# Order of work at both ends of a fused retention and MLP kernel

## The chip, the cores and the metric

The kernel runs on one core of a Trainium2 chip. The metric is the device time of one execution in microseconds (us), the median of several runs. A core has five engines that run side by side, each working through its own instructions in order: TensorE (PE, matrix products, with PEld for its weight loads), VectorE (DVE), ScalarE (ACT), GpSimd (POOL) and SyncE (SP, which here issues nearly all transfers). Transfers can also be issued from ACT; they then stand among ACT's own instructions.

## The reference

```python
# q, k, v: (8, 8, 576, 64) float32; w_in: (512, 2048); w_out: (2048, 512)
scores = (q @ k.T) / sqrt(64)                  # per batch and head
gamma = 1 - 2 ** (-5 - head)                   # decay of a head
ret = scores * where(i >= j, gamma ** (i - j), 0)
x = (ret @ v), heads side by side              # 4608 tokens x 512
h = x @ w_in
g = h * erf(softplus(h))
out = g @ w_out                                # 4608 x 512
```

The weights arrive as 64-bit floats; the kernel rounds them to float32 itself.

## The kernel before, in words

**Attention in pieces.** The 4608 tokens are cut into 36 pieces of 128 tokens. Of each batch's 576 tokens four pieces are whole, and the last 64 of two batches share a ninth piece. A piece i goes through three functions, called stages. `transposes(i)` brings q and k to the layout with the head dimension on the partitions: for pieces 0 to 7 by PE (L314) and an ACT copy (L315), from piece 8 on by DVE (L308). It also issues the q (or q and k) load of piece i + 2. `scores(i)` makes the 16 small products of q and k (L324) and masks them on DVE into the tile sT. `outputs(i)` multiplies sT with the values (L338), adds the carried state of the batch (L349), and makes this piece's contribution kv to the state (L362). DVE adds kv to the old state (`sums`), and POOL multiplies the sum with the decay (L379, the new state; for a batch's first piece DVE does it). DVE scales the output into the tile x. It also issues the k and v loads of piece i + 3. The decay that belongs to a key's position is put into the values ahead of time: `weigh_values(i)` is one multiplication on POOL (L296), which must be done before L338 and L362 of that piece. Each function is called when its turn comes, and its instructions join their engines' queues in that order.

The list `stages` holds the order of these calls. In the loop over i it appends transposes(i + 1), outputs(i), scores(i + 1), and swaps neighbours for a few i. PC is 4, so four pieces make one chunk of 512 tokens; there are nine chunks.

**Weights.** `round_weights(n)` emits n steps of the rounding of one weight part: two ACT passes, four DVE passes (L242, L246, L250, L255), two POOL passes (L256, L257), after which the next part's load is issued. The first group's eight parts (four of w_in, four of w_out) are rounded while attention starts; the last step of a w_in or w_out set makes four sums on DVE.

**The MLP.** Both matrix products use seven half-size products in place of eight, with sums of operands (named A11, S1 to S4, ... and B11, T1 to T4, ...). The hidden dimension is cut into 4 groups; for each group all nine chunks pass. `First(g, c)` makes the hidden tile of one group and chunk, `Second` multiplies it with w_out and accumulates onto an output tile o that is kept in DRAM between groups. In a `Second` the products B11, T2, T1, B22 go into one PSUM accumulator, each on top of the last, and DVE or ACT reads it out between them (`take`); B21 has an accumulator of its own, T3 and T4 share a third (`add`). Each such product is eight matmuls (L551; L445 in `First`). The very first one is done plainly with eight products (`plain`, L499), mixed among attention's stages.

**The order at the start** is written out by hand in one string: a calls the next stage, p the next plain product, w loads two weight parts, s stores chunk 0 of x, a digit emits that many rounding steps. `keep_busy(2)`, after six of the first stages, multiplies the identity with itself to keep PE at work (L631). The string's end is followed by the rest of chunk 1 and the first products of chunk 1.

**The order at the end.** In the last two blocks there is no next `First` to put between the products. The second last block runs T2, T3, T1 (`middle`), then B22, T4 (`last`); the sums of the next block are made; then B11, B21 (`first`), and the last block runs `middle` and `last`. The results of the last group go straight to the output by `store`, one transfer per piece segment, all issued by SP. Every wait here comes from data: an accumulator that must be read before PE adds to it, a buffer that must be free, a transfer that must land.

Of the kernel before, what the change touches and what calls it, by code (L numbers as in the profile page):

```python
# [15 lines left out]
ALU = mybir.AluOpType  # L16
# [31 lines left out]
def kernel(  # L48
# [42 lines left out]
    def tt(out, in0, in1, op):  # L91
        nc.vector.tensor_tensor(out=out, in0=in0, in1=in1, op=op)  # L92
# [56 lines left out]

    load(0)  # L150
    cst = cpool.tile([P, CONST_COLS], FP32, name="cst")
    nc.scalar.dma_start(out=cst, in_=consts)
    ends = [0]
    for m in (H, NP * P, NP, P, H):
        ends.append(ends[-1] + m)
# [127 lines left out]
    def x_tile():  # L283
        return xpool.tile([P, n_dc + 3, TCH], FP32, tag="x", name="x")
# [12 lines left out]

    def transposes(i):
        t = live[i] = loaded.pop(i)
        if i < SQUARES:  # L300
            weigh_values(i + 1)
        for name in "qk":
            tT = t[name + "T"] = att.tile([P, NP, P], FP32, tag=name + "T", name=name + "T")
            if i >= SQUARES:
                for _, _, n, r0 in pieces[i]:
                    a = r0 // SQ * D
                    squares = t[name + "s"][:, :, a : a + n // SQ * D].rearrange("p h (a d) -> p h a d", d=D)
                    nc.vector.transpose(  # L308
                        out=tT[:, :, r0 : r0 + n].rearrange("p h (r a) -> p h a r", r=SQ), in_=squares[:, :, :, :SQ]
                    )  # L310
            else:
                pt = ps_at.tile([P, NP, P], FP32, tag="at", name=f"pt_{name}")
                for p in range(NP):
                    nc.tensor.transpose(pt[:, p, :], flat(t[name][:, 2 * p : 2 * p + 2, :]), ident)  # L314
                nc.scalar.copy(out=tT, in_=pt)  # L315
        load(i + 2, "q")
# [14 lines left out]
    def outputs(i):  # L331
        segments = pieces[i]
        t = live.pop(i)
        seen = [(kept[b], r0, n) for b, s0, n, r0 in segments if s0 > 0]
        o = ps_at.tile([P, NP, P], FP32, tag="at", name="o")
        for p in range(NP):
            for e in range(2):
                nc.tensor.matmul(  # L338
                    o[heads[e], p, :],
                    lhsT=t["v"][:, 2 * p + e, :],  # L340
                    rhs=t["sT"][:, e, p, :],
                    start=(p == 0),
                    stop=(not seen and p == NP - 1),
                    skip_group_check=True,
                )
        for state, r0, n in seen:
            for p in range(NP):
                for r in heads:
                    nc.tensor.matmul(  # L349
                        o[r, p, r0 : r0 + n],  # L350
                        lhsT=state[r, p, :],
                        rhs=t["qT"][r, p, r0 : r0 + n],
                        start=False,
                        stop=(p == NP - 1),
                        skip_group_check=True,
                    )
        b, s0, n, _ = segments[0]
        if n == P:
            kv = ps_at.tile([P, NP, D], FP32, tag="at", name="kv")
            for p in range(NP):  # L360
                for e in range(2):
                    nc.tensor.matmul(  # L362
                        kv[heads[e], p, :],
                        lhsT=t["k"][:, 2 * p + e, :],
                        rhs=t["v"][:, 2 * p + e, :],
                        start=(p == 0),
                        stop=(p == NP - 1),
                        skip_group_check=True,
                    )
            sums = kv  # L370
            if s0 > 0:
                sums = att.tile([P, NP, D], FP32, tag="sums", name="sums")
                tt(sums, kv, kept[b], ALU.add)

            if b % 2 == 0 and s0 + P + D == S:
                new = att.tile([P, NP, D], FP32, tag="last", name="last", bufs=1)
            else:
                new = att.tile([P, NP, D], FP32, tag="state", name="state")
            (nc.gpsimd if s0 > 0 else nc.vector).tensor_tensor(out=new, in0=sums, in1=gp, op=ALU.mult)  # L379
            kept[b] = new  # L380
        load(i + 3, "kv")
        weigh_values(i + 1)
        c, at = i // PC, i % PC * P
        if (0, c) not in x:
            x[0, c] = x_tile()
        by = gq[:, :, :n].unsqueeze(2).to_broadcast([P, NP, P // n, n])
        parts = [y.rearrange("p a (m i) -> p a m i", i=n) for y in (x[0, c][:, :NP, at : at + P], o)]
        tt(parts[0], parts[1], by, ALU.mult)

    stages = [(transposes, 0), (scores, 0)]  # L390
    for i in range(len(pieces)):
        stages += [(transposes, i + 1), (outputs, i), (scores, i + 1)]
        if i in (PC - 1, PC):
            stages[-3:-1] = stages[-2], stages[-3]
    stages = [(of, i) for of, i in stages if i < len(pieces)]
    done = [0]

# [4 lines left out]
    def after_chunk(c):  # L402

        return stages.index((outputs, (c + 1) * PC - 1)) + 1
# [31 lines left out]
    class First:  # L436
# [84 lines left out]
            for j, t in enumerate((self.t1, self.t2)):  # L521
                tt(t, t, self.s[:, j], ALU.mult)

        def sums(self):
            g11, g21, g12, g22 = (t[:, j] for t in (self.t1, self.t2) for j in range(2))
            s1, s2, s3, s4 = (self.s[:, i, j] for i in range(2) for j in range(2))
            tt(s1, g12, g22, ALU.add)
            tt(s2, s1, g11, ALU.subtract)
            tt(s3, g11, g12, ALU.subtract)
            tt(s4, g21, s2, ALU.subtract)  # L530

            self.left = {B11: g11, B21: g21, T2: s2, T3: s3, T1: s1, B22: s4, T4: g22}

    class Second:


        def __init__(self, first):
            self.of = first
            self.g, self.c = first.g, first.c
            self.end = (self.g, self.c) == (n_g - 1, n_ch - 1)  # L540

        def begin(self):
            self.o = opool.tile([P, 2, 2, D_MODEL], FP32, tag="o", name="o")
            if self.g > 0:
                nc.sync.dma_start(out=self.o, in_=od[self.c])

        def product(self, b, acc, start):
            left = self.of.left[b]
            for j in range(GP):
                for tp in range(2):  # L550
                    nc.tensor.matmul(  # L551
                        acc[:, tp, :],
                        lhsT=left[:, j * TH + tp * P : j * TH + (tp + 1) * P],
                        rhs=weights["wb", self.g][:, b, j, :],
                        start=(start and j == 0 and tp == 0),
                        stop=(j == GP - 1),
                        skip_group_check=True,
                    )
# [36 lines left out]
        def last(self):  # L595
            self.product(B22, self.a, False)
            self.take(0, 1, self.a, "scalar")
            self.store(0)
            if self.end:
                self.store(1, slice(OH, D_MODEL))  # L600
            yield
            self.product(T4, self.e, False)
            self.add(1, 0, self.e)
            self.store(1, slice(0, OH if self.end else D_MODEL))
            yield

        def store(self, half, os=slice(0, D_MODEL)):
            if self.g < n_g - 1:
                nc.sync.dma_start(out=od[self.c][:, half, :, os], in_=self.o[:, half, :, os])
            else:  # L610
                for tp in range(2):
                    for b, s0, n, r0 in pieces[self.c * PC + 2 * half + tp]:
                        nc.sync.dma_start(
                            out=out[b * S + s0 : b * S + s0 + n, os], in_=self.o[r0 : r0 + n, half, tp, os]
                        )

# [27 lines left out]
    products = firsts[0].plain()  # L644


    for j, what in enumerate("aaaawaaawaa4a1a5asa1a4pa5papapa5p4apa1p4apa5a5a"):
        if what == "a":
            attend(done[0] + 1)
        elif what == "p":  # L650
            next(products)
        elif what == "s":
            store_x(0)
        elif what == "w":
            load_weights()
            load_weights()
        else:
            round_weights(int(what))
        if j < 7 and what == "a":
            keep_busy(2)  # L660
    firsts[0].softplus()
    most[0] = before_chunk(3)
    attend(after_chunk(1))
    operands_x(0, 1)
    attend(done[0] + 1)
    for _ in firsts[1].first():
        attend(done[0] + 1)
        round_weights(2)
# [2 lines left out]
    for b, nxt in zip(blocks[1:], blocks[2:] + [None]):  # L671
# [23 lines left out]
        elif n + 1 < n_s:  # L695
            firsts[n + 1].erf()
            seconds[n + 1].begin()
            run(b.middle())
            firsts[n + 1].multiply()
            run(b.last())  # L700
            firsts[n + 1].sums()
            run(nxt.first())
        else:
            run(b.middle())
            run(b.last())


# [28 lines left out]
```

## Time and profile before

| | us |
|---|---|
| median of 5 runs | 1053.4 (1052.75 to 1054.94) |
| profiled execution | 1052.97 |
| its span in the trace | 1051.2 |
| PE busy | 1030.8 (98%) |
| DVE busy | 639.6 (61%) |
| ACT busy | 378.1 (36%) |
| POOL busy | 134.6 (13%) |
| mean granted clock of PE | 0.995 |
| share of PE in the chain that ended last | 93% |

The span runs from the first instruction to the last event; the 1.8 us around it belong to the execution but not to the trace. Busy times of an engine are sums over its instructions. Idle time of an engine that is not the bound costs nothing by itself.

### The profile page before, as it was taken

How to read it: one execution, taken by the hardware profiler on the slowest of the kernel's cores; microseconds unless marked ns; L12 is line 12 of the kernel's file. 1: busy time of each engine (PE TensorE's matmuls, PEld its weight loads, DVE VectorE, ACT ScalarE, POOL GpSimd, SP SyncE). 2: the span in 40 equal slices, each digit the busy share in tenths (PEclk: the TensorE clock that was granted, in tenths of full speed). 3: DMA queues.
4: the chain of work that ended last, by engine and by line, in shares of the span. 5: the costliest groups of instructions: out<-in, count | busy, mean ns of one | idle time of the engine just before them, and what ended most of it. 6: DMA issues, size and time to landing. Idle time of an engine off the chain costs nothing.

```text
span 1051.2 us, 15690 instructions
## 1 busy us (share of the span) xinstructions
PE 1030.8 (98%) x6322; PEld 887.8 (84%) x6322; DVE 639.6 (61%) x965; ACT 378.1 (36%) x459; POOL 134.6 (13%) x130
## 2 busy tenths in 40 slices
PE   8889999999999999999999999999999999999997
PEld 7677888888888888888888888888888888888885
DVE  3679879779777654556555655555556544454444
ACT  3243231331331444443433333434443333333341
POOL 2551322221221100100001000110100000000000
PEclk9899999999999999999999999999999999999999
DMA  9989989989995534544455455553333444454432
GB/s 196 252 173 245 234 191 254 219 228 241 206 264 174 190 112 150 190 170 171 159 196 198 153 190 201 193 191 151 150 150 120 150 170 176 164 201 167 175 121 80
DMA packets 146777, 192.23 MB, mean 183 GB/s; under 512 B 96016, under 2 KB 121104, under 8 KB 138640
## 3 DMA queue, kind: packets, MB, share of 16 engines
q1 hardware_dynamic: 146560, 190.88, 61.7%
q8 instruction: 50, 0.82, 0.4%
q10 hardware_dynamic: 144, 0.34, 0.1%
q14 instruction: 23, 0.19, 0.1%
HBM read 137.70 MB, written 53.48 MB: 182 GB/s over the span
## 4 chain that ended last, share of the span: by engine, by line
PE 93%; DVE 2%; DMA 2%; SPq 1%; issue 0%; POOL 0%; ACT 0%; POOLq 0%; ACTq 0%
PE a L551 23%; PE a L445 22%; PE g L445 12%; PE g L551 11%; PE e L551 6%; PE e L445 5%; PE s L324 3%; PE o L338 3%; PE o L349 3%; PE kv L362 2%; DMA raw_v<-in_v_dram 1%; SPq L134 1%; DVE o L92 1%; DVE t L92 1%; PE p L499 1%; DVE x L92 1%
## 5 line engine op out<-in xcount | busy, mean ns | idle before, releaser
L445 PE MATMUL a<-x,wa 128*128 128x256 f32 x1120 | 266.0, 380 | 0.0
L445 PEld LDWEIGHTS a<-x,wa 128*128 128x128 f32 x1120 | 211.6, 190 | 29.4
L551 PE MATMUL a<-wb,s 128*128 128x256 f32 x864 | 205.6, 381 | 2.1 <-DVE o L92 2.1
L551 PEld LDWEIGHTS a<-wb,s 128*128 128x128 f32 x864 | 162.9, 190 | 26.1 <-DVE o L92 2.4
L92 DVE TENSOR_TENSOR o<-a,o 128x512 f32<-128x512 f32 x108 | 74.3, 688 | 109.7 <-PE a L551 104.2
L92 DVE TENSOR_TENSOR t<-g,t 128x512 f32<-128x512 f32 x70 | 48.3, 691 | 148.6 <-ACT t L475 114.5
L445 PE MATMUL g<-x,wa 128*128 128x256 f32 x560 | 133.3, 381 | 0.1
L445 PEld LDWEIGHTS g<-x,wa 128*128 128x128 f32 x560 | 105.6, 190 | 15.8 <-DVE o L92 0.9
L256 POOL TENSOR_TENSOR wraw<-wraw 128x512 f32<-128x512 f32 x32 | 33.3, 1040 | 465.5 <-DVE wraw L255 244.0
L470 ACT COPY t<-a 128x512 f32<-128x512 f32 x35 | 20.5, 586 | 190.3 <-PE a L445 190.3
L92 DVE TENSOR_TENSOR t<-t,s 128x1024 f32<-128x1024 f32 x72 | 87.2, 1252 | 0.0
L514 ACT ACTIVATE s<-t 128x1024 f32<-128x1024 f32 x72 | 72.1, 1048 | 31.7 <-DVE t L92 31.6
L481 ACT COPY t<-a 128x512 f32<-128x512 f32 x35 | 20.5, 586 | 150.5 <-PE a L445 150.5
L518 ACT ACTIVATE s<-s 128x1024 f32<-128x1024 f32 x72 | 72.1, 1049 | 0.4
L551 PE MATMUL a<-wb,t 128*128 128x256 f32 x288 | 68.6, 381 | 0.0
L551 PE MATMUL g<-wb,s 128*128 128x256 f32 x288 | 68.6, 381 | 0.0
L551 PE MATMUL e<-wb,t 128*128 128x256 f32 x288 | 68.6, 381 | 0.0
L551 PE MATMUL g<-wb,t 128*128 128x256 f32 x288 | 68.2, 380 | 0.0
L445 PE MATMUL e<-x,wa 128*128 128x256 f32 x280 | 66.7, 381 | 0.0
L551 PEld LDWEIGHTS g<-wb,t 128*128 128x128 f32 x288 | 54.6, 190 | 7.5
L551 PEld LDWEIGHTS e<-wb,t 128*128 128x128 f32 x288 | 54.3, 190 | 7.7
L551 PEld LDWEIGHTS g<-wb,s 128*128 128x128 f32 x288 | 54.3, 190 | 7.6
(77 smaller groups left out, 1195.5 us busy)
## 6 DMA issues: line engine op xcount, KB each, us to landing
x<-xd SPq DMA_DIRECT2D x24, 1792.0 KB, 10.8
od<-o SPq DMA_DIRECT2D x54, 512.0 KB, 4.2
o<-od SPq DMA_DIRECT2D x27, 1024.0 KB, 7.1
xd<-x SPq DMA_DIRECT2D x8, 1792.0 KB, 7.5
raw_qs<-in_q_dram SPq DMA_DIRECT2D x96, 112.0 KB, 4.8
raw_ks<-in_k_dram SPq DMA_DIRECT2D x96, 112.0 KB, 4.5
raw_k<-in_k_dram SPq DMA_DIRECT2D x64, 128.0 KB, 4.5
raw_v<-in_v_dram SPq DMA_DIRECT2D x64, 128.0 KB, 4.6
```

The lines of the kernel that those rows point to most:

```text
L92: nc.vector.tensor_tensor(out=out, in0=in0, in1=in1, op=op)
L256: nc.gpsimd.tensor_tensor(out=r_f, in0=high_f, in1=r_f, op=ALU.mult)
L324: nc.tensor.matmul(ps[e][:, p, :], lhsT=t["kT"][heads[e], p, :], rhs=t["qT"][heads[e], p, :], start=True, stop=True)
L338: nc.tensor.matmul(o[heads[e], p, :], lhsT=t["v"][:, 2 * p + e, :], rhs=t["sT"][:, e, p, :], start=(p == 0), stop=(not seen and p == NP - ...
L349: nc.tensor.matmul(o[r, p, r0 : r0 + n], lhsT=state[r, p, :], rhs=t["qT"][r, p, r0 : r0 + n], start=False, stop=(p == NP - 1), skip_group_ ...
L362: nc.tensor.matmul(kv[heads[e], p, :], lhsT=t["k"][:, 2 * p + e, :], rhs=t["v"][:, 2 * p + e, :], start=(p == 0), stop=(p == NP - 1), skip ...
L445: nc.tensor.matmul(acc[:, j * TH : (j + 1) * TH], lhsT=weights["wa", self.g][:, a, d, j * P : (j + 1) * P], rhs=x[self.g, self.c][a][:, d, :],
L470: nc.scalar.copy(out=self.t1[:, 1], in_=self.a)
L481: nc.scalar.copy(out=self.t2[:, 0], in_=self.a)
L514: nc.scalar.activation(self.s[:, j], t, AF.Softplus)
L518: nc.scalar.activation(self.s[:, j], self.s[:, j], AF.Erf)
L551: nc.tensor.matmul(acc[:, tp, :], lhsT=left[:, j * TH + tp * P : j * TH + (tp + 1) * P], rhs=weights["wb", self.g][:, b, j, :], start=(sta ...
```

## The change

At the start: `transposes` no longer weighs values; `outputs` scales its output into x first, then makes the state, and only then weighs the values of the next piece. The table of constants is loaded by SP behind the six loads of piece 0 instead of by ACT. For i of 2 and 6 scores(i + 1) comes ahead of outputs(i), and for i of 7 outputs(i) comes ahead of transposes(i + 1), as it did for 3 and 4. The string of the start is rewritten; `keep_busy(2)` gets a letter of its own, k, and three of them stand between scores(4) and outputs(4). The number of rounding steps stays 44.

At the end: a new method `rest` takes the place of `middle` and `last` in the last two blocks. It runs T2, T3, T1, T4 and then B22 in two halves of four matmuls, each half added and stored by itself. T3 is added to o at once. Some stores are issued from ACT. The sums of the last block are made in two parts, with the first product B11 and its take between them.

```diff
     load(0)
     cst = cpool.tile([P, CONST_COLS], FP32, name="cst")
-    nc.scalar.dma_start(out=cst, in_=consts)
+    nc.sync.dma_start(out=cst, in_=consts)
...
     def transposes(i):
         t = live[i] = loaded.pop(i)
-        if i < SQUARES:
-            weigh_values(i + 1)
...
+        c, at = i // PC, i % PC * P
+        if (0, c) not in x:
+            x[0, c] = x_tile()
+        by = gq[:, :, :n].unsqueeze(2).to_broadcast([P, NP, P // n, n])
+        parts = [y.rearrange("p a (m i) -> p a m i", i=n) for y in (x[0, c][:, :NP, at : at + P], o)]
+        tt(parts[0], parts[1], by, ALU.mult)
+        if n == P:
             sums = kv
             if s0 > 0:
                 sums = att.tile([P, NP, D], FP32, tag="sums", name="sums")
...
             kept[b] = new
         load(i + 3, "kv")
         weigh_values(i + 1)
-        c, at = i // PC, i % PC * P
-        if (0, c) not in x:
-            x[0, c] = x_tile()
-        by = gq[:, :, :n].unsqueeze(2).to_broadcast([P, NP, P // n, n])
-        parts = [y.rearrange("p a (m i) -> p a m i", i=n) for y in (x[0, c][:, :NP, at : at + P], o)]
-        tt(parts[0], parts[1], by, ALU.mult)
...
-        if i in (PC - 1, PC):
+        if i in (PC - 1, PC, 2 * PC - 1):
             stages[-3:-1] = stages[-2], stages[-3]
+        elif i in (PC - 2, 2 * PC - 2):
+            stages[-2:] = stages[-1], stages[-2]
...
-        def sums(self):
+        def sums(self, parts=(0, 1)):
...
+            if 0 in parts:
+                tt(s1, g12, g22, ALU.add)
+                tt(s2, s1, g11, ALU.subtract)
+            if 1 in parts:
+                tt(s3, g11, g12, ALU.subtract)
+                tt(s4, g21, s2, ALU.subtract)
...
+        def rest(self):
+            e = ps_e.tile([P, 2, OH], FP32, tag="g", name="g2")
+            self.product(T2, self.a, False)
+            self.take(1, 0, self.a, "vector")
+            yield
+            self.product(T3, e, True)
+            self.add(1, 1, e)
+            self.store(0, slice(0, OH), nc.scalar)
+            yield
+            self.product(T1, self.a, False)
+            self.take(1, 1, self.a, "vector")
+            yield
+            self.product(T4, e, False)
+            self.add(1, 0, e)
+            self.store(1)
+            yield
+            for tp in range(2):
+                self.product(B22, self.a, False, (tp,))
+                dst = self.o[:, 0, tp, OH:]
+                tt(dst, self.a[:, tp, :], dst, ALU.add)
+                self.store(0, slice(OH, D_MODEL), nc.sync if tp else nc.scalar, (tp,))
+            yield
...
-    for j, what in enumerate("aaaawaaawaa4a1a5asa1a4pa5papapa5p4apa1p4apa5a5a"):
+    for what in "akakakakwakakawaa1a3a15asaakkka5p5apapap5p4apa1p4apaa55":
...
+        elif what == "k":
+            keep_busy(2)
...
-        if j < 7 and what == "a":
-            keep_busy(2)
     firsts[0].softplus()
     most[0] = before_chunk(3)
-    attend(after_chunk(1))
+    attend(after_chunk(1) + 1)
     operands_x(0, 1)
-    attend(done[0] + 1)
...
             seconds[n + 1].begin()
-            run(b.middle())
+            rest = b.rest()
+            for _ in range(3):
+                next(rest)
             firsts[n + 1].multiply()
-            run(b.last())
-            firsts[n + 1].sums()
-            run(nxt.first())
+            run(rest)
+            firsts[n + 1].sums((0,))
+            first = nxt.first()
+            next(first)
+            firsts[n + 1].sums((1,))
+            run(first)
         else:
-            run(b.middle())
-            run(b.last())
+            run(b.rest())
```

More of the change, by code (lines that the diff above doesn't have):

```diff
@@ L522, in multiply @@
                 tt(t, t, self.s[:, j], ALU.mult)
-        def sums(self):
+        def sums(self, parts=(0, 1)):
             g11, g21, g12, g22 = (t[:, j] for t in (self.t1, self.t2) for j in range(2))
             s1, s2, s3, s4 = (self.s[:, i, j] for i in range(2) for j in range(2))
[L527 to L530, printed above, removed]
+            if 0 in parts:
[4 more added lines that the diff above has]
+                tt(s4, g21, s2, ALU.subtract)
             self.left = {B11: g11, B21: g21, T2: s2, T3: s3, T1: s1, B22: s4, T4: g22}
@@ L539, in __init__ @@
             self.g, self.c = first.g, first.c
-            self.end = (self.g, self.c) == (n_g - 1, n_ch - 1)
         def begin(self):
@@ L545, in begin, with product @@
                 nc.sync.dma_start(out=self.o, in_=od[self.c])
-        def product(self, b, acc, start):
+        def product(self, b, acc, start, tps=(0, 1)):
             left = self.of.left[b]
             for j in range(GP):
-                for tp in range(2):
+                for tp in tps:
                     nc.tensor.matmul(
@@ L598, in last @@
             self.store(0)
-            if self.end:
-                self.store(1, slice(OH, D_MODEL))
             yield
@@ L603, in last, with store @@
             self.add(1, 0, self.e)
-            self.store(1, slice(0, OH if self.end else D_MODEL))
+            self.store(1)
             yield
-        def store(self, half, os=slice(0, D_MODEL)):
+        def rest(self):
[12 more added lines that the diff above has]
+            self.add(1, 0, e)
+            self.store(1)
+            yield
[5 more added lines that the diff above has]
+            yield
+        def store(self, half, os=slice(0, D_MODEL), queue=nc.sync, tps=(0, 1)):
             if self.g < n_g - 1:
@@ L610, in store @@
             else:
-                for tp in range(2):
+                for tp in tps:
                     for b, s0, n, r0 in pieces[self.c * PC + 2 * half + tp]:
-                        nc.sync.dma_start(
+                        queue.dma_start(
                             out=out[b * S + s0 : b * S + s0 + n, os], in_=self.o[r0 : r0 + n, half, tp, os]
```

## The prediction

> Short names: T(i), S(i), O(i) are the calls transposes(i), scores(i), outputs(i); W(i) is weigh_values(i), one 1.04 us multiply on POOL. Lines L... are those of the kernel before.
>
> **What bounds the kernel now.** First the page: TensorE is busy for 1030.8 of 1051.2 us, so an edit pays only where PE is idle, runs slowly, or does filler, or after its last product.
>
> ```profile
> span 1051.2 us, 15690 instructions
> PE 1030.8 (98%) x6322; PEld 887.8 (84%) x6322; DVE 639.6 (61%) x965; ACT 378.1 (36%) x459; POOL 134.6 (13%) x130
> ```
>
> Then the windows view, in 10 us steps, for where the missing 20.4 us lie: 1.8 in 0:10, 1.3 in 10:20, 1.7 in 20:30, 2.8 in 30:40, 3.6 in 60:70, 0.5 and 0.8 in the next two, 0.8 in 1020:1030, 0.55 in 1030:1040, 6.3 from 1040. That is 20.2: between 90 and 1020 us there is next to nothing. Both ends are all that counts.
>
> The timeline shows the first large stall. POOL takes work in order; T(3) has queued W(4) ahead of the state of O(2).
>
> ```profile
> 30.37 1.04 POOL L296 TENSOR_TENSOR raw_v<-raw_v,cst 128x512 f32<-128x512 f32 x1 [8.65 <-DMA raw_v<-in_v_dram]
> 31.37 0.61 POOL L379 TENSOR_TENSOR state<-sums,cst 128x256 f32<-128x256 f32 x1
> ...
> 32.04 1.97 PE L349 MATMUL o<-qT,state 64*64 64x128 f32 x16 [2.54 <-POOL state L379]
> ```
>
> W(4) waited for a value tile that landed at 30.2, the state waited behind it though its sums were ready at 26.2, and PE waited 2.54 us. The 16 products then took 1.97 us instead of 1.09: the clock. Cutting the windows view into 3.41 us pieces (columns: stretch, sum, then busy us of PE, PEld, DVE, ACT, POOL, then PEclk, DMA share, GB/s) shows what halves it.
>
> ```profile
> 26.58:30.00 3.42, 1.72 (x20) 1.04 (x17) 3.32 (x8) 0.00 (x0) 0.00 (x0) 1.00 1.07 210
> 30.00:33.41 3.41, 1.37 (x14) 1.38 (x16) 0.34 (x1) 0.00 (x0) 2.96 (x4) 0.50 1.18 212
> 33.41:36.83 3.42, 3.42 (x30) 2.70 (x26) 1.02 (x2) 0.58 (x1) 3.34 (x4) 0.50 1.08 188
> 64.13:67.55 3.42, 2.22 (x42) 1.79 (x38) 2.14 (x4) 3.39 (x5) 1.12 (x1) 1.00 0.85 181
> 67.55:70.96 3.41, 0.75 (x8) 0.51 (x10) 3.31 (x7) 1.26 (x2) 2.19 (x4) 1.00 1.07 225
> 70.96:74.37 3.41, 3.41 (x34) 2.75 (x30) 3.34 (x6) 0.00 (x0) 1.79 (x2) 0.50 1.28 196
> ```
>
> A piece with PE busy for 1.72 or less is followed by one at 0.50; one with 2.22 is not. A halved piece full of work costs 1.7 us.
>
> The second stall (66.35 to 70.04, 3.69 us) is DVE's: O(7) needs the mask of S(7), and that stood behind a weight rounding on DVE. From 65.4 to 102 DVE is busy 36 of 36.6 us, so there it is as much the bound as PE. Keep this for the sum.
>
> At the end, the timeline of the last products and stores:
>
> ```profile
> 1041.06 0.69 DVE L92 TENSOR_TENSOR o<-a,o 128x512 f32<-128x512 f32 x1 [2.76 <-PE a L551]
> 1041.81 1.99 PE L551 MATMUL a<-wb,s 128*128 128x256 f32 x8 [0.79 <-DVE o L92]
> 1043.64 1.89 PE L551 MATMUL g<-wb,t 128*128 128x256 f32 x8
> 1044.56 4.23 SPq L613 DMA_DIRECT2D out_dram<-o  x8
> 1045.56 0.69 DVE L92 TENSOR_TENSOR o<-g,o 128x512 f32<-128x512 f32 x1 [1.03 <-PE g L551]
> ```
>
> Two things: B22 goes into the accumulator that T1 just filled, so PE waits 0.79 us for DVE to read it; and eight stores stand in one queue, which is busy to 1048.8, 2.5 us after the last add. The last one lands 2.4 us later: 1051.2.
>
> **The end.** In the last two blocks the order is now T2, T3, T1, T4, B22. T4 goes to the other accumulator and covers the read of T1's. Before, from T1's end of the block before last (1027.11) to the last product's (1045.54) there are 18.43 us for nine products; a product in an unbroken stream takes 1.726 (rows of 1.73), nine take 15.53. So 2.90 us are stalls: 0.79 and 0.79 behind T1, 0.55 at T2, and the 0.25 that each first product after a stall takes longer (1.97 to 1.99). Do they go? The multiplies come behind T1's take: 1027.82 to 1030.2 on DVE (their Erf inputs are ready at 1027.0 and 1028.0), T4's add and the two half adds to 1031.7, s1 and s2 to 1032.95, the take of B11 to 1033.6. B21, the fourth product, ends at 1027.11 + 4 x 1.726 = 1034.0: T2 has its s2 and its accumulator 0.4 us before that. That cover of 0.4 is the thinnest; without it T2 stalls up to 0.55 again. So the last product ends at 1042.64, not 1045.54.
> The tail: B22 comes in two halves. The last add is 128x256 (0.42, as the sums<-kv rows that read the same shape), done at 1043.1. T4's add ends at 1041.7, then SP issues three stores at 0.44 to 0.6 each, to 1043.0 to 1043.5; one half store goes to ACT, where nothing is queued after the Erf. The last store is issued from 1043.25 to 1043.75 and lands 2.4 later (rows: 1.9 to 3.6) at 1046.15. Gain: 1051.2 - 1046.1 = **5.1 us**, bounds 3.9 (landing 3.6) and 5.6 (landing 1.9). Stores on ACT's queue are not in the trace; its one transfer, cst, landed in 3.4 us, and its stores are not last.
>
> **The start, constants.** cst leaves ACT at 0.73 and is issued by SP at about 4.5, ahead of load(1). From 5 to 10 us the transfers run at a steady 219 GB/s, and the six of load(0) with cst landed by 7.76. The same bytes land by then in the new order, so cst arrives at 7.8 to 8.4 and W(0) starts there (before: 7.80). k of piece 0 lands up to 1.4 us sooner (cst's queue took 14.1% of 16 engines over 10 us); but T(2) waits at 16.32 for its own q. All later queries and values stand behind one more issue of 0.5 on SP. I take 0, bounds -0.6 and +0.5.
>
> **The start, first stall.** S(3) now precedes O(2), and O(3) follows O(2) at once; W(3) is queued behind the state of O(2). Walk: T(3) ends at 22.45 as before; S(3) waits for the kT copy (23.34), runs 23.4 to 24.5; O(2) takes 2.66, to 27.2. DVE: masks to 25.8, three rounding operations (0.43+0.43+0.69) to 27.4, x<-o to 28.05, sums to 28.45. POOL: state to 29.1, W(3) to 30.15. PE idles 3.0 us, a new wait in the old one's place. O(3) from 30.2; with the next 3.41 us at half clock it ends at 34.4 (before 35.06), without at 33.0. T(4) ends 35.3, its kT 36.05, S(4) 37.2. Three keep_busy(2), 0.43 each, fill 1.3 us while DVE masks (to 38.5): covered. W(4), behind the weights on POOL, is done at 36.6: covered. O(4), p1, T(5), p2 end at 44.5; the same work before ended at 45.05. Gain 0.5; at full clock 0 to 1.4 more.
>
> **The start, second stall.** From p1 to p8 PE is solid in both. S(7) now runs right behind p8, its mask lands in DVE's idle 61.4 to 65.4, so O(6) and O(7) no longer wait for a rounding. But O(7) follows O(6) directly, and W(7) stands behind state(6): sums 0.42 + state 0.61 + W 1.04 + latencies 0.2 = 2.3 us of idle PE instead of 3.69. From there DVE decides. It has the 1.28 of two masks done before its dense stretch; it reaches sums(6) at 66.4 against 66.31. So it is 1.2 ahead until about 102. PE can use more than that only where it has slack: the new order puts O(9) and O(10) one product (1.73) behind their old places, so their masks are needed later. Walk, DVE's times being the old ones less 1.2 plus what was moved ahead: T(9) stands behind two weight sums and an add (2.1), done 83.16 - 1.2 + 2.1 = 84.1, so S(9) starts then; S1 and B11 end at 88.6; O(9)'s mask is there at 90.35 - 1.2 = 89.2; O(9) and B21 end at 91.9; T(10), behind one rounding step and an add (1.1), 92.35 - 1.2 + 1.1 = 92.2; S(10), S4, A22 to 96.8; O(10)'s mask, behind another step and add, 97.84 - 1.2 + 1.1 = 97.7, its first half at 97.1; O(10) from 97.2 to 99.9. Then all is done that before was done at 103.1. Gain **3.2 us**, the 0.5 included; bounds -1 (DVE loses its lead and more) and +4.8 (DVE keeps up with a PE that saves the difference of the stalls, 1.4, and a half clock at both places, 1.7 each).
> Moving x<-o ahead of sums costs nothing: it runs while PE does kv (0.62), and behind 100 us the state is needed a block later.
> One price on POOL: state and W now run beside DVE's rounding. An L246 beside POOL's L257 took 1.40 instead of 0.43. Before, the two roundings at 66 to 73 had three such hits already (1.15, 0.98, 1.39), so I add none.
> The Trainium skill (SBUF — State Buffer, SBUF: two separate sides) speaks against that: it has DVE and GpSimd locking a shared port pair for whole instructions, the loser fully blocked. By it, state and W(7) could hold DVE 0.61 + 1.04 = 1.65 longer, and the start would gain 1.55 (total 1046.8).
>
> **Sum.** 5.1 + 3.2 = 8.3. The profiled execution took 1052.97 (span 1051.2 and 1.8 around it): 1044.7. The median, 1053.4, lies 0.4 above it: **1045.1**.
>
> **Rivals.**
> Start gives nothing: both new waits eat what the old ones gave, DVE's lead is lost. Only the end: 1053.4 - 5.1 = 1048.3. For it: DVE is solid from 65 to 102; against: masks move into real idle time.
> Start gives all: no halved clock, DVE keeps up: 4.8 + 5.1 = 9.9, 1043.5. For it: a wait that straddles two 3.41 us pieces leaves both above the 1.7 mark.
> The tail hides it: the last store lands as late as the queue allows, and only stalls go (2.90 + 0.27), with the start as forecast: 1053.4 - 3.2 - 3.2 = 1047.0. With no gain at the start either, 1050.2.
> Slower: values behind the state. The W(3) and W(7) waits come on top, since the old stalls were landings and DVE in truth and stay: 3.0 + 2.3 idle, 1.7 each for the clock, 1.3 of filler, 10 us; less 5.1, 1058. It decides if the start loses more than 5.1; for it: O(2)/O(3) and O(6)/O(7) leave no product between. Against: v of piece 4 no longer holds up a state.
>
> **How the numbers follow.** Chances: forecast 0.48 (its own range 1043.8 to 1047.0), start gives nothing or the tail hides it 0.25, start gives all 0.15, losses that just eat the end's gain 0.05, slower 0.07. Range 1042.5 to 1050.2: from all upper bounds together (4.8 + 0.5 + 5.6 = 10.9) to the case in which only the stalls at the end go. About 0.2% (2.1 us) is what a measurement of this kernel can tell. Faster 0.88, same 0.05, slower 0.07.
>
> **What would show it.** Right: no PE wait at the two B22 and at T2; last add about 3 us and last landing about 5 us nearer to the start; PE waits of 3 and 2.3 us at o<-sT,raw_v of O(3) and O(7), released by POOL raw_v, the clock at 0.50 behind at least one; DVE solid from 66 to 101. Wrong: a PE wait for DVE of over 1 us between 75 and 100, a start that is later at its first L551 product (91.9 before), or a last store that lands over 3.6 us after its add.

## The result, and the profile after

The median after is **1050.92 us** (1049.49 to 1053.16, 27 runs) against 1053.18 us for the kernel before (48 runs): a ratio of **0.9978 [0.9972, 0.9983]**, 2.3 us or 0.22% less. The profiled execution took 1049.72 us with a span of 1047.9, against 1052.97 and 1051.2. So the profiled pair differs by 3.3 us where the forecast had 8.3, and the median of 1050.92 lies above the forecast's range (1042.5 to 1050.2). The page of the kernel after, its first lines:

```profile
span 1047.9 us, 15748 instructions
PE 1028.7 (98%) x6334; PEld 886.8 (85%) x6334; DVE 644.9 (62%) x967; ACT 378.4 (36%) x459; POOL 134.0 (13%) x130
```

DVE is busier by 5.3 us with practically the same work, and by the windows view all of that lies in the first 120 us; it will matter for the start.

**The end.** From the timeline of the kernel after, rows of PE and DVE from the take behind T1 of the block before last (columns: start, duration, engine, line, operation; in brackets the idle time before and what ended it):

```profile
1026.52 0.69 DVE L92 TENSOR_TENSOR o<-a,o 128x512 f32<-128x512 f32 x1 [1.03 <-PE a L553]
1027.12 2.35 DVE L92 TENSOR_TENSOR t<-t,s 128x1024 f32<-128x1024 f32 x2
1028.04 1.03 PE L553 MATMUL a<-wb,s 128*128 128x256 f32 x4
1029.39 0.68 DVE L92 TENSOR_TENSOR o<-g,o 128x512 f32<-128x512 f32 x1
1029.99 0.41 DVE L92 TENSOR_TENSOR o<-a,o 128x256 f32<-128x256 f32 x1
1030.46 1.13 PE L553 MATMUL a<-wb,s 128*128 128x256 f32 x4 [1.39 <-DVE o L92]
...
1043.33 1.13 PE L553 MATMUL a<-wb,s 128*128 128x256 f32 x4 [0.52 <-DVE o L92]
1044.50 0.42 DVE L92 TENSOR_TENSOR o<-a,o 128x256 f32<-128x256 f32 x1 [1.22 <-PE a L553]
```

The first half of B22 runs without a wait, as forecast: T4 covers the read of T1's accumulator. But the second half waits until DVE has added the first (the x1 of 128x256 at 1029.99), and that add stands on DVE behind the two multiplies (2.35) and T4's add (0.68): 1.39 us of idle PE in the block before last, 0.52 in the last block, where no multiplies stand ahead. The wait at T2 is gone.

The yardstick used below runs from that take behind T1 to the end of the span: 1051.2 - 1027.13 = 24.07 us before, 1047.9 - 1026.52 = 21.38 after. The end gained **2.7 us**, not 5.1. It is a good yardstick: kernels with the same end agree in it whichever start they have (24.09 with the end of before and the new start; 21.38 again with the end of after and the old start), though their starts differ by microseconds.

**The start.** The two new waits of O(3) and O(7), and a third, at T(6), where the forecast had PE without a gap, from the timeline of the kernel after:

```profile
30.55 1.16 PE L336 MATMUL o<-sT,raw_v 128*64 128x128 f32 x16 [3.15 <-POOL raw_v L296]
...
47.97 0.63 PE L312 MATMUL pt_q<-ident,raw_q 128*128 128x128 f32 x4 [0.96 <-DMA raw_q<-in_q_dram]
...
69.03 1.33 PE L336 MATMUL o<-sT,raw_v 128*64 128x128 f32 x16 [2.58 <-POOL raw_v L296]
```

All waits of PE from 20 to 102 us (for whom, us in total, times, longest), first after, then before:

```profile
PE o L336 <- POOL raw_v L296: 5.7, 2, 3.2
PE s L322 <- ACT kT L313: 1.6, 2, 0.8
PE pt_q L312 <- DMA raw_q<-in_q_dram: 1.0, 1, 1.0
PE s L322 <- DVE kT L306: 0.8, 1, 0.8
PE o L336 <- issue: 0.5, 1, 0.5
```

```profile
PE o L338 <- DVE sT L92: 6.0, 6, 3.7
PE o L349 <- POOL state L379: 2.5, 1, 2.5
PE s L324 <- ACT kT L315: 0.7, 1, 0.7
```

They add up to 9.6 us after and 9.2 before: the waits have changed places, not size.

The four operand sums (DVE) with what POOL does beside them, first after, then before:

```profile
75.84 4.82 DVE L92 TENSOR_TENSOR x<-x 128x512 f32<-128x512 f32 x4
76.15 1.06 POOL L384 TENSOR_TENSOR state<-sums,cst 128x256 f32<-128x256 f32 x1
77.17 2.94 POOL L296 TENSOR_TENSOR raw_v<-raw_v,cst 128x512 f32<-128x512 f32 x2
80.58 1.27 DVE L92 TENSOR_TENSOR sT<-s,tri 128x512 f32<-128x512 f32 x2
```

```profile
76.10 3.88 DVE L92 TENSOR_TENSOR x<-x 128x512 f32<-128x512 f32 x4
...
79.91 1.27 DVE L92 TENSOR_TENSOR sT<-s,tri 128x512 f32<-128x512 f32 x2
```

By the forecast DVE should have been 1.2 us ahead here. It starts the sums 0.26 us ahead, and the mask of S(8) behind them comes 0.67 us later than before.

### The profile page after: what moved, and what is told of

Same layout as the page of the kernel before. It is cut to its first block, busy times and chain, and to the rows that moved or that the text cites. A ratio compares the mean times of both kernels' runs of the same rounds, so it can differ in the third digit from the quotient of the medians.

```text
span 1047.9 us, 15748 instructions
## 1 busy us (share of the span) xinstructions
PE 1028.7 (98%) x6334; PEld 886.8 (85%) x6334; DVE 644.9 (62%) x967; ACT 378.4 (36%) x459; POOL 134.0 (13%) x130
## 4 chain that ended last, share of the span: by engine, by line
PE 92%; DVE 4%; DMA 2%; SPq 1%; issue 1%; POOL 0%; ACT 0%; DVEq 0%; ACTq 0%; POOLq 0%
PE a L553 24%; PE a L446 22%; PE g L446 12%; PE g L553 12%; PE e L553 6%; PE e L446 5%; PE s L322 3%; PE o L336 3%; PE o L347 2%; PE kv L360 2%; DVE t L92 1%; DMA raw_q<-in_q_dram 1%; DVE o L92 1%; SPq L134 1%; DVE x L92 1%
## 5 line engine op out<-in xcount | busy, mean ns | idle before, releaser
L92 DVE TENSOR_TENSOR o<-a,o 128x512 f32<-128x512 f32 (+1 forms) x110 | 74.6, 678 | 107.1 <-PE a L553 101.6
L553 PEld LDWEIGHTS a<-wb,t 128*128 128x128 f32 x288 | 54.4, 190 | 7.6
```

Source lines behind the costliest of these rows:

```text
L553: nc.tensor.matmul(acc[:, tp, :], lhsT=left[:, j * TH + tp * P : j * TH + (tp + 1) * P], rhs=weights["wb", self.g][:, b, j, :], start=(sta ...
```

## The experiments

All kernels below were compared with the kernel before on the same chip; "after" is the changed kernel. The diffs are excerpts against after. The first two experiments take the change apart into its two ends.

**The new end alone.** Start of before, end of after.

```diff
-    nc.sync.dma_start(out=cst, in_=consts)
+    nc.scalar.dma_start(out=cst, in_=consts)
...
-        if i in (PC - 1, PC, 2 * PC - 1):
+        if i in (PC - 1, PC):
...
-    for what in "akakakakwakakawaa1a3a15asaakkka5p5apapap5p4apa1p4apaa55":
+    for j, what in enumerate("aaaawaaawaa4a1a5asa1a4pa5papapa5p4apa1p4apa5a5a"):
...
```

> The start of before with the new end. Theory A (from the trace of after: the end gave 2.7 us there, because each second half of B22 waited 1.39 and 0.52 us for the add of the first half): 2.7 us faster than before. Rival B (the end gave the forecast 5.1 and the start lost about 3): 5 us faster than before.

Measured: 1050.3 against 1052.5, ratio 0.9982 [0.9973, 0.9991], by the ratio 1.9 us less (0.9 to 2.8). The yardstick's 2.7 lies inside, the forecast's 5.1 outside.

**The new start alone.** Start of after, with `middle` and `last` of before.

```diff
-            rest = b.rest()
-            for _ in range(3):
-                next(rest)
+            run(b.middle())
             firsts[n + 1].multiply()
-            run(rest)
+            run(b.last())
...
```

> The new start with the end of before. Theory A: the trace of after is 0.6 us ahead by the end of the start, and its median is 2.3 ahead of before in all, so the start alone lies between 0.6 us faster and 0.4 us slower than before. Rival B (the end gave 5.1): 3 us slower. Rival C (the forecast): 3.2 us faster.

Measured: 1053.03 against 1052.5, ratio 1.0007 [0.9998, 1.0015]. The whole gain that can be seen is the end's; the new start lies between 0.2 us faster and 1.6 us slower. Its profiled execution (1052.15) shows a span 0.8 us shorter than before's, but it is the fastest of its 11 runs: a single pair of traces misleads here. How much so is seen at a landmark behind the start, the first T3 of a `Second`. Two kernels with the very same start as before, each with T3 in the timeline and the first 100 us in the windows view (columns: stretch, sum, busy us of PE, PEld, DVE, ACT, POOL, then PEclk, DMA share, GB/s): first the new end alone, then the new end with B22 whole (an experiment further down):

```profile
107.04 1.89 PE L552 MATMUL g<-wb,s 128*128 128x256 f32 x8
0.00:100.00 100.00, 88.28 (x850) 73.87 (x852) 63.77 (x107) 31.91 (x50) 35.13 (x39) 0.93 0.99 214
```

```profile
103.25 1.89 PE L552 MATMUL g<-wb,s 128*128 128x256 f32 x8
0.00:100.00 100.00, 87.45 (x897) 72.88 (x898) 69.31 (x111) 33.45 (x51) 37.41 (x41) 0.98 1.01 219
```

The kernel before had T3 at 106.06. The same instructions in the same order arrive up to 3.8 us apart, and the clock goes with it: in 1 us steps the windows view shows four pieces of 3.41 us at 0.50 in the first of these traces, one in the second, three in the kernel before. So the start is judged by medians only, and traces of it serve for single waits.

**B22 whole.** One product of eight matmuls and one add, the stores still on two queues.

```diff
-            for tp in range(2):
-                self.product(B22, self.a, False, (tp,))
-                dst = self.o[:, 0, tp, OH:]
-                tt(dst, self.a[:, tp, :], dst, ALU.add)
-                self.store(0, slice(OH, D_MODEL), nc.sync if tp else nc.scalar, (tp,))
+            self.product(B22, self.a, False)
+            self.add(0, 1, self.a)
+            self.store(0, slice(OH, D_MODEL), nc.scalar, (0,))
+            self.store(0, slice(OH, D_MODEL), nc.sync, (1,))
```

> After, with B22 as one product of eight matmuls and one 128x512 add in both last blocks; the two stores stay on their two queues. Theory A (the split itself makes PE wait, since the second half goes into the accumulator tile that the first half's add still reads): no PE wait there any more, 1.39 + 0.52 and two times 0.1 to 0.25 of refilling gained, 0.27 given back by the longer last add: 1.9 to 2.4 us faster than after, 4.2 to 4.7 faster than before. Rival (the tail is set by the stores that SP issues ahead): at most 0.5 us faster than after.

Measured: 1048.6 against 1052.5, 0.9966 [0.9953, 0.9978]. No product of the last two blocks waits for DVE any more: from the take behind T1 to the last add PE is unbroken. The timeline of this kernel:

```profile
1026.03 0.69 DVE L92 TENSOR_TENSOR o<-a,o 128x512 f32<-128x512 f32 x1 [1.04 <-PE a L553]
...
1041.57 0.69 DVE L92 TENSOR_TENSOR o<-a,o 128x512 f32<-128x512 f32 x1 [1.03 <-PE a L553]
```

15.54 us lie between the take behind T1 and the last add, the nine products of 1.726 that the forecast had counted (15.53); in the kernel after the same distance is 1044.50 - 1026.52 = 17.98. The 2.44 in excess are the two waits (1.91) and 0.53 more around them, where the stream of products breaks off and starts again. Of that, 0.27 goes back since the last add is whole (0.69, not 0.42), and 0.6 since the span ends 3.54 us behind the last add instead of 2.98; the two last stores are now issued at the same time. That leaves 19.77 by the yardstick, a gain of 4.3. The median's gain, 3.6 us, is less than the 4.2 to 4.7 expected, but its interval (2.5 to 4.9) holds them.

**Both halves issued ahead of both adds.** Here the halves and the two stores stay, and only the order of issue changes.

```diff
             for tp in range(2):
                 self.product(B22, self.a, False, (tp,))
+            for tp in range(2):
                 dst = self.o[:, 0, tp, OH:]
```

> After, with both halves of B22 issued ahead of both half adds. If the wait between the halves is the write into a tile that an add still reads (theory A), PE waits no more at all at B22, and the last add ends about 2.1 us nearer to the start of T2 of the block before last than in after. If it is the first half's product that is slow to finish or DVE's own backlog, a wait of 0.5 us or more stays.

Measured in one run: 1048.39 us, span 1046.6. No PE wait at B22, and from the take behind T1 to the end of the span 1046.6 - 1026.73 = 19.87. The half size was not the trouble; an add between the two halves was.

**The corrected end by itself.** The last diff together with that of the new end alone.

> The start of before, the end of the change, but both halves of B22 are issued ahead of the two half adds; the stores stay as in the change, one last half store behind the other. Theory (the forecast's 5.1 us for the end was right but for the wait between the halves): the kernel with the change's end alone gained 2.2 us in the median; without the 1.39 and 0.52 us waits and their refill it gains 2.0 to 2.4 more, 4.2 to 4.8 in all: 0.9954 to 0.9960. Rival (the stores or the landing take the rest, as where B22 is whole): 3.3 to 3.9 us, 0.9963 to 0.9969. Profile: no wait of PE at the products of B22, and from DVE's take behind T1 of the block before last to the end of the span 19.5 to 20 us (24.1 in before, 21.4 in the change).

Measured: 1048.17 against 1053.32, ratio **0.9952 [0.9938, 0.9966]**, 5.1 us less [3.6, 6.5]. In the chain of this kernel that ended last (columns: start, duration, what), B22 and the B11 behind it are one unbroken stretch of 16 matmuls, twice 1.726:

```profile
1028.73 1.73 PE g L552 x8
1030.46 3.45 PE a L552 x16
1033.91 1.73 PE e L552 x8
```

By the yardstick: 1048.7 - 1028.77 = 19.93, a gain of 4.1 in the trace. The median (5 runs) cannot tell between the two expectations, and the trace lies between the 4.2 of the one and the 3.9 of the other. Two halves are worth no more than B22 whole (19.77).

**B22 whole with the start of before.** The diff of B22 whole together with that of the new end alone.

> The start of before with the new end and B22 whole. Theory A (the new start gives nothing that can be measured; the split cost 2 us): 4 us faster than before, within 0.7 us of whole_last. Rival C (the new start gives 1 us or more): over 1 us slower than whole_last.

Measured: 1048.53 against 1052.3, 0.9963 [0.9949, 0.9977]; B22 whole with the new start had 0.9966. Again the two starts cannot be told apart, and the yardstick is the same, 19.77.

**Values weighed ahead of the state.** W(i + 1) goes back in front of the state in `outputs`, the rest stays.

```diff
         tt(parts[0], parts[1], by, ALU.mult)
+        if i < SQUARES:
+            weigh_values(i + 1)
         if n == P:
             sums = kv
```

> After, with the values of pieces 1 to 8 weighed ahead of the state in the same outputs call instead of behind it. Theory D (the two waits of PE for POOL raw_v, 3.15 and 2.58 us, are the order of POOL's queue, and DVE is delayed there by POOL): both waits fall to 1 us or less, which wait for the state, and 1.5 to 3 us come back. Rival E (DVE is the bound from 66 to 102 us whatever POOL does, and loads hold pieces 4 to 6): the waits go but at most 0.5 us is gained.

Measured: 1050.44 against 1052.5, 0.998 [0.9971, 0.9989], no better than after. The waits of PE in this kernel, 20 to 102 us (columns: who, for whom, us in total, times, longest):

```profile
PE s L322 <- DVE kT L306: 3.9, 1, 3.9
PE pt_q L312 <- DMA raw_q<-in_q_dram: 2.2, 1, 2.2
PE o L347 <- POOL state L386: 1.6, 2, 1.1
PE s L322 <- DVE x L92: 1.6, 1, 1.6
PE s L322 <- ACT kT L313: 0.8, 1, 0.8
PE o L336 <- POOL raw_v L296: 0.2, 1, 0.2
```

The waits for POOL's values fall from 5.7 to 0.2 us, and as much comes back, mostly as waits for DVE's transposed keys (3.9 in place of 0.8) and for the queries of piece 6 (2.2 in place of 1.0). So W(i + 1) behind the state had no price that the median shows: PE, running ahead, meets DVE or the loads next.

**The rounding earlier.** The last ten rounding steps are moved forward by a few calls.

```diff
-...p4apa1p4apaa55
+...p45apa5p5apaa
```

> After, with the last three weight parts rounded earlier: two of them beside O(5) and the plain products at 52 to 62 us, where DVE is idle for 4 of 10 us, instead of in the dense stretch from 66.9 to 73.6. Theory E (DVE, 6.7 us of rounding in that stretch, decides the start): T(8), the four operand sums and the masks behind them come 4 to 6 us earlier, no wait of PE for DVE kT, 1.5 to 3.5 us faster than after. Rival D (the POOL waits decide): the wait of 2.6 us for POOL raw_v at O(7) stays and with it the time, within 0.6 us of after.

Measured: 1050.76 against 1052.39, 0.9981 [0.9971, 0.999], no gain over after. Now O(7) waits 4.4 us, as the mask, x and sums of O(6) stand behind the rounding on DVE, and state and W(7) behind another on POOL.

**B22 whole, values ahead and rounding earlier, all three.** The edits are those shown above.

> After, with B22 whole, the values weighed ahead of the state, and the rounding earlier as in round_early. Theory E: with DVE out of the way the weighing pays too: whole_last's 1048.6 less 1.5 to 3.5, and up to 2 us more: 1043 to 1047, the fastest of all. Rival (loads of pieces 6 to 9 are the next bound): 1047.5 to 1048.6.

Measured: 1048.37 against 1052.39, **0.9957 [0.9944, 0.9969]**. That is the gain of B22 whole, within the intervals. Its waits are 3.8 for POOL's values at O(7) and 2.2 for the queries.

**The rounding spread.** With B22 whole, values ahead and W(7) two pieces ahead, the last steps are spread over more calls.

```diff
+            if i == 5:
+                weigh_values(7)
...
-...p4apa1p4apaa55
+...p45apa5papaa5
```

> After, with B22 whole, values weighed ahead of the state (those of piece 7 already in outputs(5)), one weight part rounded beside O(5), one before O(6), and one left behind O(6). Theory E (DVE and POOL, one queue each, set the start; a rounding must stand neither in the dense stretch nor ahead of the mask of S(7)): no wait for POOL raw_v at O(7), the wait for DVE kT at S(8) 1.5 us or less, first T3 product (105.3 in after) at 102.5 to 104, time 1046 to 1048. Rival (the time only moves from wait to wait, the loads of pieces 6 to 9 are behind it): 1048.4 to 1049.

Measured: 1048.4 against 1052.3, 0.9969 [0.9958, 0.998], the rival's value. The wait for values is down to 0.2 and T3 comes at 102.63 in the trace, as expected, with one piece at half clock; the median does not follow. The longest wait left is that of T(6) for its load, from the timeline of this kernel:

```profile
47.90 1.09 PE L312 MATMUL pt_q<-ident,raw_q 128*128 128x128 f32 x4 [2.56 <-DMA raw_q<-in_q_dram]
```

**Without W(8) and W(9).** The multiplications of two pieces, which fall beside the four operand sums, are left out.

```diff
             weighed.add(i)
+            if i in (8, 9):
+                return
```

> After, without the multiplications W(8) and W(9) on POOL (so pieces 8 and 9 have unweighed values); nobody on PE waits for these two in the trace of after, they only run beside DVE's operand sums. Theory P (POOL and DVE hold each other up): the four operand sums fall from 4.82 us to 3 or less, S(9) and O(9) come 1 to 2 us earlier, 0.5 to 1.5 us faster than after. Rival (the sums are slow for another reason): 4.8 us as before, no change.

Measured: 1050.43 against 1052.39, 0.9977 [0.9968, 0.9986]. In the trace of this kernel the four sums take 3.13 us instead of 4.82:

```profile
76.01 3.13 DVE L92 TENSOR_TENSOR x<-x 128x512 f32<-128x512 f32 x4
76.32 1.07 POOL L386 TENSOR_TENSOR state<-sums,cst 128x256 f32<-128x256 f32 x1
```

With nothing of POOL's beside them, in the kernel with all three edits, they take 2.58. So POOL's two multiplications hold DVE up by 1.7 us here; that the median doesn't follow says that these 1.7 us alone are not what the start's time hangs on.

**Constants from ACT again.**

```diff
-    nc.sync.dma_start(out=cst, in_=consts)
+    nc.scalar.dma_start(out=cst, in_=consts)
```

> After, with the constants loaded from ACT's queue again. The forecast's step (no gain, no loss) expects no change to after. Rival (constants behind the first loads come later, 8.64 against 4.15 us, and hold up W(0) and the first mask): 0.5 to 1 us faster than after.

Measured: 1050.83 against 1052.3, 0.9987 [0.9978, 0.9996], overlapping with after's 0.9978 and on its slower side. The late constants cost nothing that can be seen.

## Why the forecast was wrong, step by step

**The end: the step "B22 comes in two halves".** Right were the terms that it removes: no wait at T2, none at the first matmuls of B22, and nine products take 15.54 us once nothing stands between the halves. The last store, too, landed 2.98 us after the last add ended, for 3.05 forecast. Wrong was that the second half follows the first at once, which the step took for granted. The walk ordered DVE's work (take, multiplies, T4's add, two half adds) correctly, but asked only when B21 and T2 find their operands, and not whether the second half of B22 may start while the first is read. It is made to wait, 1.39 and 0.52 us, 2.44 with the refills: 5.1 - 2.4 = 2.7, which is what the yardstick shows. With both halves issued before the adds the end gains 4.1 in the trace and 5.1 [3.6, 6.5] in the median; that the median meets the forecast's 5.1 is luck, with an interval that wide. Even in that order the forecast is 0.9 too high by the trace: 0.3 for the last adds (0.76 for both, in place of 0.42 for one) and 0.6 for the last store, which lands 3.63 us after them instead of 3.05.

The wait is between PE's second half and DVE's add of the first. A reason to order such accesses stands in the Trainium skill (PSUM — Partial Sum Buffer, PSUM bank collisions raise a hardware error): engines must be kept apart by bank, not by address, since hardware does not arbitrate. An accumulator here is 512 float32 in each partition, and the page gives a bank 2 KiB, which is the same size. Whether the wait comes from that or from both halves being one tile, and what would happen without it, no run here shows.

**The start: the steps "so I add none" and "from p1 to p8 PE is solid in both".** Forecast 3.2, measured nothing (1.0007 [0.9998, 1.0015]). The new waits themselves came nearly as forecast: O(3) waited 3.15 (forecast 3.0), O(7) 2.58 (2.3). The constants came at 8.64, later than the 7.8 to 8.4 forecast, at no price that the median shows. Two steps failed.

First, "so I add none", and with it "1.2 ahead until about 102". Beside POOL, L246 and L250 of one rounding took 0.72 and 1.42, where the kernel before needed 1.15 and 0.98 (even), those of the next 1.15 and 1.66 for 1.39 and 0.69 (0.73 more), and the four sums 4.82 for 3.88 (0.94 more): 1.67 us. The forecast took the hits that were there already as covering the new ones, and did not look at the operand sums. This is not one trace's accident: the five rows together take 9.8 us in the new start alone, in B22 whole and in the halves ahead of the adds too, and 6.3 to 8.1 in the four traces with the old start.

The sum that the forecast drew from the Trainium skill and set aside (SBUF — State Buffer, SBUF: two separate sides) was 1.65, and the match with 1.67 is luck. It had DVE held beside state(6) and W(7); there L246 and L250 lose nothing against before (2.14 for 2.13). The time is lost later, beside the next rounding on POOL and beside a state and two W. Nor do the four sums grow by all of POOL's work beside them: 2.24 more than the 2.58 they take alone, against 4.0 of POOL.

Second, "from p1 to p8 PE is solid in both": T(6) waits 0.96 for its queries. The walk did not look at SP's queue. T(6) asks for them at 47.0 us instead of 49.63, but they are issued at 41.54, against 41.63 before, behind the store of x. A lead of 2.6 us becomes one of 1.66. Where POOL's waits are taken away, this wait grows to 2.2 or 2.6. It differs between traces, though: in the new start alone the queries are issued at 40.75 and T(6) does not wait, but S(8) waits 2.3 for DVE's keys in place of 0.8.

What each of the two costs is not shown: taking away POOL's waits, or 1.7 us of the held-up sums, won nothing by itself. What the runs do show is that the waits of PE do not get fewer (9.6 to 10.5 us in four traces with the new start, 8.7 to 10.6 in four with the old).

**The clock.** The start's worth also goes through the granted clock. The windows view of the kernel after, in pieces of 3.41 us set so that the halved one falls into one row (columns: stretch, sum, then busy us of PE, PEld, DVE, ACT, POOL, PEclk, DMA share, GB/s):

```profile
25.51:28.92 3.41, 1.89 (x38) 1.41 (x34) 3.34 (x8) 1.26 (x2) 0.33 (x1) 1.00 1.18 210
28.92:32.34 3.42, 1.79 (x28) 1.62 (x30) 3.32 (x4) 0.00 (x0) 3.34 (x4) 1.00 0.97 218
...
66.47:69.88 3.41, 0.85 (x15) 0.85 (x16) 3.31 (x6) 2.44 (x3) 1.91 (x2) 1.00 1.02 218
69.88:73.29 3.41, 3.41 (x39) 2.64 (x34) 3.31 (x5) 0.00 (x0) 2.44 (x2) 0.50 1.21 203
```

The longer wait, 3.15 us at O(3), lies across two pieces, leaves PE busy for 1.89 and 1.79 in them, and costs no clock. The shorter one, 2.58 us at O(7), lies inside one piece, leaves 0.85, and the next piece runs at 0.50. That agrees with the forecast's mark (1.72 halves, 2.22 does not) and, if the mark is the same in both kernels, narrows it to between 1.72 and 1.79. Where the pieces fall differs from run to run, and with it the time of the same program: with the old start, one, three, four and four halved pieces go with T3 at 103.25, 106.06, 107.04 and 107.69. With the new start, three traces have one halved piece each and T3 at 104.95 to 105.56, a fourth has two and 104.85. So with one halved piece the new start is about 2 us later than the old, not 3.2 earlier; the old start, however, has only one such trace. The medians fit that. In the runs of one comparison the new start alone had a mean clock of 0.9968 (11 runs), the kernel before 0.9939 (27 runs); but among runs of a clock from 0.994 to 0.996 the new start took 1053.6 (mean of 4 runs), the kernel before 1052.2 (15). The new start is throttled less and takes longer at the same clock, and the two cancel. The groups are small: that the sum is near nothing is shown by the medians, its split only by these means and traces. The forecast was walked from one trace of the old start, with three halved pieces.

**The rivals.** "Start gives nothing" came true for the start, and on top of it half of the end's gain was lost, by a mechanism that no rival had. "The tail hides it" was wrong (the last store landed as forecast); that its 1050.2 with no gain at the start comes nearest to the median is luck. "Values behind the state" was right on the waits (3.15 and 2.58 us) and wrong on their price: without them the time stayed the same.

**Open** stays the start's sign (between 0.2 us faster and 1.6 slower), and which resource sets its time.

## What to carry to other kernels

Before an instruction is split so that its first part can be read early, ask whether the program lets the second part write while the first is read; if both lie in one accumulator, issue all parts first and read them afterwards. A stall removed early in a stage is worth only what the next late resource leaves of it (here nothing, where POOL's 5.7 us of waits went), so walk every queue that feeds the stage, the loads included, up to the point where both orders meet. Where the same start scatters by 4 us between traces, compare medians of the halves of a change, not one pair of profiles, and count the halved pieces in the trace that a forecast starts from.

## What was not expected of the hardware

Last stores that are issued on two queues at the same time land later: 2.6 us after the end of SP's last issue where ACT's ends 1.6 us earlier (after), 3.1 to 3.3 us where both end within 0.4 us (B22 whole, and both kernels with the adds behind), 2.4 where SP alone issues (before). The cause was not isolated.

POOL pays too when it meets DVE: a multiplication W takes 1.47 us beside the operand sums and 1.04 alone, a state 1.06 and 0.61.
